# Pairs of token tiles on one Trainium2 core: first-layer sums formed by TensorE in PSUM instead of by VectorE

## The chip, the cores and the metric

One core of one Trainium2 chip (trn2). The metric is the device time of one launch in microseconds (us). The kernel before takes 569.94 us (median of three runs, 569.79 to 570.28).

## The reference

The program is one retention block (linear attention with decay) whose output, 1536 tokens by 512 values, goes through two MLPs of the same size. The change is in the MLPs alone. Cut to what matters:

```python
def _moe_ref(x, w_in, w_out):              # x 1536x512, w_in 512x2048, w_out 2048x512
    h = np.maximum(x @ w_in, 0.0)
    return (h * h @ w_out).astype(np.float32)

def _moe2_ref(x, w_in, w_out):
    h = x @ w_in
    g = np.maximum(0.01 * h, h)
    return (g @ w_out).astype(np.float32)

def reference(**kwargs):
    ...
    return _moe2_ref(x=_moe_ref(x=x, **moe_kwargs), **moe2_kwargs)
```

The weights arrive as 64-bit floats, and the kernel turns them into 32-bit ones itself.

## The kernel before

**Stages.** After the retention block (up to about 62 us of the span) the two MLPs run one after the other, `l` = 0 (squared Relu) and `l` = 1 (leaky Relu). Each is cut into four slices `s` of 512 hidden values, and a stage (l,s) takes all 1536 tokens through its slice: the first layer (`first`, `first_pair`), the activation, and the second layer (`second`, `second_last`), whose results of the slices are added up in DRAM (`keep`, the tiles `spill`). Tokens stand in three tiles of 512 columns. Every fp32 operand is split into a high and a low part of TensorE's type float32r (`split`, L69 copy on ScalarE, L70 remainder on VectorE), and a product of two operands is three matmuls: high by high, high by low, low by high. All matmuls of the MLPs are issued at one line, L531, in `three`; each streams 512 columns.

**Pairs.** In seven of the eight stages the first layer of token tiles 0 and 1 is done by `first_pair` as a 2x2 block product with seven products instead of eight (Winograd's form of Strassen's scheme). The 256 hidden values of each half `h` are the blocks A11 to A22 of the weights (128 rows of the result each), the two tiles' halves are the blocks B11 to B22; S1 to S4 are sums of weight blocks (`weight_sums`, L426 to L431, tiles `sw`), T1 to T4 sums of token blocks (`token_sums`, tiles t2, t3, t4, T1 in place of a block of tile 1). One product is six matmuls into one PSUM bank. A stage has 14 products (seven for each of two halves), always both halves of a product one behind the other. I number the pair stages 1 to 7: (0,1), (0,2), (0,3), (1,0), (1,1), (1,2), (1,3).

**What follows a product.** Before, ScalarE copies A11·B11 out of its bank (L607) into a scratch tile `s1`, and five adds on VectorE for each half (`plus`, L601) form the sums in scratch tiles from the other banks; TensorE itself adds two products into one bank three times (S3·T3 on S2·T2, A12·B21 on A11·B11, S4·B22 on S1·T1). `put` then activates each of the four result blocks (i,t) of a half. For l = 0 a block in scratch gets max(x,0)·x on VectorE (L464), the high part by a copy on ScalarE (L465); a block read from its bank gets Relu, square, square on ScalarE (L467 to L469). For l = 1 both parts come from leaky Relus on ScalarE (L471, L472). The low part is always a subtraction on VectorE (L473), into g0l or g1l, which the second layer reads as weights of tokens 0 or 1.

**Order.** TensorE's order is written out by hand: it is that of the program. SP's (the DMA queue of loads) is by hand in the retention block alone. VectorE, ScalarE and GpSimd get their order from a scheduler that goes by priority, mostly the place in the program; `tc.high_priority(offset=400)` around the adds and around `put` for tile 0 lets them go ahead of work up to that far earlier. An engine takes its instructions strictly in that order, so a waiting instruction holds what is queued behind it.

**Weight conversion.** Between the products the program converts the next weights. A generator `converting` does one piece of 128x1024: ScalarE takes the absolute value (L111) of the raw 64-bit words once their load has landed, VectorE works on it in four steps (L112, L113, L115, L118), of which L118 is the last to read the raw buffer; `fetch` then loads the next piece into it (two raw buffers, 1 MB for a load, issued on SP at L66). For first-layer weights the sums L426 to L429 follow. Once the place in the program allows it (`opened`), ScalarE copies the high part (L135) and VectorE forms the low one (L137). `convert` takes one step of this at every `yield True` of the MLP code; at `yield False` none. So the `yield` values in `first_pair` set where in the program the conversion steps stand:

```python
        for room in part:
            if room is not False:
                convert()
```

Of scratch tiles (`plain`, tag f) there are nine, of the tiles hb that a piece is converted in two, and all eight PSUM banks rotate through `bank()`.

## Time and profile before

| | |
|---|---|
| median of three runs (lowest, highest) | 569.94 us (569.79, 570.28) |
| the profiled execution's own time | 569.29 us |
| its span in the trace | 567.3 us |
| TensorE busy, matmuls | 558.4 us, 98% of the span |
| VectorE busy | 415.6 us, 73% |
| ScalarE busy | 290.6 us, 51% |
| GpSimd busy | 89.8 us, 16% |
| share of TensorE in the chain that ended last | 95%, L531 alone 88% |
| granted clock of TensorE in the profile's slices | nine tenths or more of full speed in all 40 |
| read from and written to HBM | 49.81 and 22.03 MB |

The span is the stretch from the first to the last instruction in the trace; the execution's own time is 1.99 us longer. The stages begin, in us from the start of the span, at 128.02, 190.58, 253.14, 315.83, 378.39, 440.95 and 503.51 for the seven pairs.

### The profile page before, as it was taken

How to read it: one execution, taken by the hardware profiler on the slowest of the kernel's cores; microseconds unless marked ns; L12 is line 12 of the kernel's file. 1: busy time of each engine (PE TensorE's matmuls, PEld its weight loads, DVE VectorE, ACT ScalarE, POOL GpSimd, SP SyncE). 2: the span in 40 equal slices, each digit the busy share in tenths (PEclk: the TensorE clock that was granted, in tenths of full speed). 3: DMA queues.
4: the chain of work that ended last, by engine and by line, in shares of the span. 5: the costliest groups of instructions: out<-in, count | busy, mean ns of one | idle time of the engine just before them, and what ended most of it. 6: DMA issues, size and time to landing. Idle time of an engine off the chain costs nothing.

```text
span 567.3 us, 8188 instructions
## 1 busy us (share of the span) xinstructions
PE 558.4 (98%) x3159; PEld 470.7 (83%) x3159; DVE 415.6 (73%) x613; ACT 290.6 (51%) x450; POOL 89.8 (16%) x101
## 2 busy tenths in 40 slices
PE   7999999999999999999999999999999999999997
PEld 6889888888888888888888888888888888888897
DVE  3678899999955596819999996729563673629877
ACT  2344689553673445733557565454562374436510
POOL 3759100000113102120000000000203011220132
PEclk9999999999999999999999999999999999999999
DMA  8998544536337627394514224442729514460434
GB/s 177 243 211 189 188 148 150 186 149 189 98 47 193 104 76 148 85 194 112 185 29 139 75 91 132 121 175 77 133 61 210 115 20 55 66 83 1 166 133 149
DMA packets 68472, 72.37 MB, mean 128 GB/s; under 512 B 39753, under 2 KB 43857, under 8 KB 68433
## 3 DMA queue, kind: packets, MB, share of 16 engines
q1 hardware_dynamic: 60848, 58.87, 34.7%
q0 software_dynamic: 6912, 12.59, 15.3%
q8 instruction: 25, 0.41, 0.3%
q10 hardware_dynamic: 672, 0.39, 0.2%
q14 instruction: 15, 0.11, 0.1%
HBM read 49.81 MB, written 22.03 MB: 127 GB/s over the span
## 4 chain that ended last, share of the span: by engine, by line
PE 95%; DMA 2%; POOL 1%; SPq 1%; ACT 1%; issue 0%; DVE 0%; ACTq 0%; POOLq 0%
PE ps L531 88%; PE ps L299 2%; PE ps L350 1%; PE ps L282 1%; DMA raw<-in_moe_w_in 1%; PE ps L348 1%; PE ps L323 1%; DMA q<-in_q 1%; SPq L66 1%; POOL kd L317 0%; POOL qS L292 0%; ACT kT L286 0%; ACT qT L286 0%; PE ps L273 0%; ACT xhi L69 0%
## 5 line engine op out<-in xcount | busy, mean ns | idle before, releaser
L650 POOL DMA_DIRECT2D spill<-f x48 | 42.5, 886 | 404.6 <-ACT f L646 258.9
L531 PE MATMUL ps<-xhi,w1h 128*128 128x512 f32 x216 | 84.1, 390 | 0.0
L531 PE MATMUL ps<-xhi,w1l 128*128 128x512 f32 x216 | 84.0, 389 | 0.0
L531 PE MATMUL ps<-xlo,w1h 128*128 128x512 f32 x216 | 84.0, 389 | 0.0
L646 ACT COPY f<-ps 128x512 f32<-128x512 f32 x72 | 42.0, 584 | 74.4 <-PE ps L531 74.0
L137 DVE TENSOR_TENSOR w2l<-hb,w2h 128x1024 fp32r<-128x1024 f32 x16 | 19.6, 1227 | 61.4 <-ACT w2h L135 61.0
L601 DVE TENSOR_TENSOR f<-ps,f 128x512 f32<-128x512 f32 x70 | 46.4, 692 | 6.4 <-PE ps L531 6.3
L473 DVE TENSOR_TENSOR g0l<-f,g0h 128x512 fp32r<-128x512 f32 x52 | 35.3, 691 | 21.3 <-ACT f L472 14.6
L531 PEld LDWEIGHTS ps<-xhi,w1h 128*128 128x128 f32 x216 | 40.5, 188 | 8.5 <-issue 0.2
L531 PEld LDWEIGHTS ps<-xhi,w1l 128*128 128x128 f32 x216 | 40.5, 188 | 8.5
L531 PEld LDWEIGHTS ps<-xlo,w1h 128*128 128x128 f32 x216 | 40.5, 188 | 8.3
L111 ACT ACTIVATE hb<-raw 128x1024 f32<-128x1024 f32 x32 | 36.7, 1148 | 15.3 <-DMA raw<-in_moe_w_in 6.5
L118 DVE SCALAR_TENSOR_TENSOR hb<-raw,hb 128x1024 uint16<-128x1024 uint32 x32 | 43.8, 1367 | 0.2
L531 PE MATMUL ps<-g0l,w2h 128*128 128x512 f32 x112 | 43.7, 390 | 0.0
L531 PE MATMUL ps<-g0h,w2h 128*128 128x512 f32 x112 | 43.6, 389 | 0.0
L531 PE MATMUL ps<-g0h,w2l 128*128 128x512 f32 x112 | 43.6, 389 | 0.0
L531 PE MATMUL ps<-t,sw 128*128 128x512 f32 x168 | 40.3, 389 | 0.0
L531 PE MATMUL ps<-w2l,g0h 128*128 128x512 f32 (+1 forms) x104 | 39.6, 381 | 0.0
L531 PE MATMUL ps<-w2h,g0l 128*128 128x512 f32 (+1 forms) x104 | 39.6, 381 | 0.0
L531 PE MATMUL ps<-w2h,g0h 128*128 128x512 f32 (+1 forms) x104 | 39.6, 381 | 0.0
L115 DVE SCALAR_TENSOR_TENSOR hb<-raw,hb 128x1024 uint32<-128x1024 uint32 x32 | 39.2, 1224 | 0.4
L531 PEld LDWEIGHTS ps<-t,sw 128*128 128x128 f32 x168 | 31.5, 188 | 6.5
(188 smaller groups left out, 1227.4 us busy)
## 6 DMA issues: line engine op xcount, KB each, us to landing
raw<-in_moe_w_in SPq DMA_DIRECT2D x16, 1024.0 KB, 5.7
raw<-in_moe_w_out SPq DMA_DIRECT2D x16, 1024.0 KB, 4.8
spill<-f POOLq DMA_DIRECT2D x48, 256.0 KB, 4.1
spill<-f SPq DMA_DIRECT2D x24, 256.0 KB, 3.1
k<-in_k SPq DMA_DIRECT2D x12, 256.0 KB, 4.6
q<-in_q SPq DMA_DIRECT2D x12, 256.0 KB, 5.2
v<-in_v SPq DMA_DIRECT2D x12, 256.0 KB, 5.7
f<-spill SPq DMA_DIRECT2D x12, 256.0 KB, 2.7
```

Of the source, the lines that this page charges most:

```text
L66: return nc.sync.dma_start(dst, src)
L111: nc.scalar.activation(hf, w_hi.bitcast(F32), AF.Abs)
L115: yield ve.scalar_tensor_tensor(out=hb, in0=w_hi, scalar=0xC0000000, in1=hb, op0=ALU.bitwise_and, op1=ALU.bitwise_or)
L118: step = ve.scalar_tensor_tensor(out=half, in0=w_lo, scalar=2.0 ** -29, in1=half, op0=ALU.mult, op1=ALU.add)
L137: yield ve.tensor_tensor(out=lo, in0=hf, in1=hi, op=ALU.subtract)
L282: nc.tensor.transpose(ps[:, p, :], src[:, 2 * p:2 * p + 2, :].rearrange("s h d -> s (h d)"), ident)
L299: nc.tensor.matmul(raw_scores[i][par][:, p, :], kT[i][r, p, :], qT[i][r, p, :], start=True, stop=True)
L473: nc.vector.tensor_tensor(out=glo, in0=r, in1=ghi, op=ALU.subtract)
L531: nc.tensor.matmul(ps, a, b, start=start and n == 0, stop=stop and n == len(ops) - 1, skip_group_check=again)
L601: ve.tensor_tensor(out=out, in0=ps[h, where], in1=other, op=ALU.add)
L646: nc.scalar.copy(f, src)
L650: nc.gpsimd.dma_start(dst, f, accum_op=ALU.add)
```

## The change

In `first_pair` the scratch sum s1 and the five adds go. `seed` copies a finished product from its bank straight into another bank on ScalarE (L606 of the changed kernel): A11·B11 into bank B, and, once S2·T2 has been added on it there, the sum of the two into bank D. TensorE then accumulates in the seeded banks (`start` false): S2·T2 and S3·T3 and later A22·T4 in B, S4·B22 in D. ScalarE copies S1·T1 into a scratch tile p5 (L619), and two adds for each half are left on VectorE (L610): B + p5 into r22 and D + p5 into p5. The order of the products becomes A11·B11, S1·T1, S2·T2, S3·T3, A12·B21, A22·T4, S4·B22, in place of A11·B11, S2·T2, A22·T4, S3·T3, S1·T1, A12·B21, S4·B22. The block (1,0), once made by an add in scratch, is now read from bank B; for l = 0 that goes by a Relu and a square on ScalarE (L464, L465) and a product r·r on VectorE (L466). A few tiles change their names (`home`, the tag in `weight_sums`), and in the last stage "sums" is opened two products later. In the changed file the old lines L464 to L473 of `activate` stand at L468 to L477, L531 at L535, L646 at L650.

```diff
--- before.py
+++ after.py
@@ -141,7 +141,7 @@
             rb = cv.tile([P, 4 * CW], U32, tag="rb", name="rb")
             w = hf.rearrange("p (k i m f) -> p k i m f", k=2, i=2, m=2)
             blocks = {(i, j): w[:, j, i] for i in range(2) for j in range(2)}
-            yield from weight_sums(key, f"t{h + 2}", blocks, rb.bitcast(F32))
+            yield from weight_sums(key, f"t{2 * h + 2}", blocks, rb.bitcast(F32))
 
     def convert(pin=False):
         for piece in list(at_work):
@@ -448,7 +448,7 @@
                 split(xhi[1][:, j], xlo[1][:, j], a)
                 continue
             if j == 0:
-                tag = {2: "t2", 4: "t3", 3: "t4"}[n]
+                tag = f"t{n}"
                 tt[n] = late.tile([P, 2, 2, TT], F32R, tag=tag, name=tag)
             split(tt[n][:, 0, j], tt[n][:, 1, j], src)
 
@@ -459,8 +459,12 @@
                 nc.vector.tensor_tensor(out=of[k], in0=xhi[t][:, k], in1=xlo[t][:, k], op=ALU.add)
         token_sums(j)
 
-    def activate(l, src, r, ghi, glo):
-        if l == 0 and src is r:
+    def activate(l, src, r, ghi, glo, product=False):
+        if l == 0 and product:
+            nc.scalar.activation(r, src, AF.Relu)
+            nc.scalar.square(ghi, r)
+            nc.vector.tensor_tensor(out=r, in0=r, in1=r, op=ALU.mult)
+        elif l == 0 and src is r:
             nc.vector.scalar_tensor_tensor(out=r, in0=src, scalar=0.0, in1=src, op0=ALU.max, op1=ALU.mult)
             nc.scalar.copy(ghi, r)
         elif l == 0:
@@ -475,7 +479,7 @@
 
 
     whole, tsum = {}, {}
-    home = ("t4", "sw0", "sw1")
+    home = ("t3", "sw0", "sw1")
 
     def by_blocks(x):
         return x.rearrange("q (h j) (p t c) -> q j t h p c", j=2, p=2, t=2)
@@ -576,7 +580,7 @@
         }
         for n in (2, 3, 4):
             x[f"T{n}"] = (tt[n][:, 0], tt[n][:, 1])
-        ps, s1, s2, r22 = {}, {}, {}, {}
+        ps, p5, r22 = {}, {}, {}
 
         def product(h, where, a, b, start=True):
             if start:
@@ -594,49 +598,50 @@
                 if last:
                     activate_last(t, m, src)
                 else:
-                    activate(l, src, r, g[t][0][:, m], g[t][1][:, m])
-
-        def plus(h, out, where, other):
+                    activate(l, src, r, g[t][0][:, m], g[t][1][:, m], (i, t) == (1, 0))
+
+        def seed(h, where, other):
+            ps[h, where] = bank()
             with tc.high_priority(offset=400):
-                ve.tensor_tensor(out=out, in0=ps[h, where], in1=other, op=ALU.add)
+                nc.scalar.copy(ps[h, where], ps[h, other])
+
+        def plus(h, out, where):
+            with tc.high_priority(offset=400):
+                ve.tensor_tensor(out=out, in0=ps[h, where], in1=p5[h], op=ALU.add)
 
         both = range(2)
         for h in both:
-            b = product(h, "A", "A11", "B11")
-            s1[h] = plain()
-            nc.scalar.copy(s1[h], b)
+            product(h, "A", "A11", "B11")
+            seed(h, "B", "A")
             yield True
         for h in both:
-            product(h, "B", "S2", "T2")
-            s2[h] = plain()
-            plus(h, s2[h], "B", s1[h])
+            p5[h] = plain()
+            nc.scalar.copy(p5[h], product(h, "C", "S1", "T1"))
             yield True
         for h in both:
-            product(h, "D", "A22", "T4")
+            product(h, "B", "S2", "T2", False)
+            seed(h, "D", "B")
             yield True
-        if last:
-            opened.add(("sums", l, s))
         for h in both:
             product(h, "B", "S3", "T3", False)
             r22[h] = plain()
-            plus(h, r22[h], "B", s1[h])
-            plus(h, s1[h], "D", r22[h])
-            put(h, s1[h], s1[h], 1, 0)
-            yield last
-        for h in both:
-            product(h, "C", "S1", "T1")
-            plus(h, r22[h], "C", r22[h])
+            plus(h, r22[h], "B")
             yield True
         for h in both:
             put(h, product(h, "A", "A12", "B21", False), plain(), 0, 0)
             yield last
         for h in both:
-            product(h, "C", "S4", "B22", False)
-            plus(h, s2[h], "C", s2[h])
+            put(h, product(h, "B", "A22", "T4", False), plain(), 1, 0)
+            yield last
+        if last:
+            opened.add(("sums", l, s))
+        for h in both:
+            product(h, "D", "S4", "B22", False)
+            plus(h, p5[h], "D")
             yield last
         for h in both:
             put(h, r22[h], r22[h], 1, 1)
-            put(h, s2[h], s2[h], 0, 1)
+            put(h, p5[h], p5[h], 0, 1)
         if last:
             sums_last(0)
             sums_last(1)
```

The number of matmuls, of loads and of stores is the same in both. The next listings show how the order of instructions moves, before and then changed, with the tile numbers of the two programs (they differ between them) and the engines each instruction waits for.

ScalarE in the fourth pair stage (1,0), first before, then changed, then the matmuls of TensorE in the changed kernel that wait there. ps_3062 is bank A of half 0, ps_3069 bank B; ps_3075 and ps_3082 are those of half 1; ps_3113 and ps_3124 are bank D, ps_3088 and ps_3098 bank C of the two halves; raw_2949 and raw_3016 are the two raw buffers.

```order
L607 COPY f_3069<-ps_3062 128x512 [waits PE_49,Activation_49]
L135 CAST w2h_3071<-hb_2983 128x1024 [waits DVE_49]
L607 COPY f_3082<-ps_3075 128x512 [waits PE_49]
L69 CAST xhi2_2972<-f_3036 128x512 [waits DVE_49]
L111 ACTIVATE hb_3084<-raw_2949 128x1024 [waits DMAHW4_49,DVE_49,Activation_49]
L111 ACTIVATE hb_3124<-raw_3016 128x1024 [waits DMAHW6_49,DVE_49,Activation_49]
L471 ACTIVATE g0h_3058<-f_3069 128x512 [waits DVE_49]
```

```order
L606 COPY ps_3069<-ps_3062 128x512 [waits PE_49]
L135 CAST w2h_3071<-hb_2983 128x1024 [waits DVE_49]
L606 COPY ps_3082<-ps_3075 128x512 [waits PE_49]
L69 CAST xhi2_2972<-f_3036 128x512 [waits DVE_49]
L111 ACTIVATE hb_3084<-raw_2949 128x1024 [waits DMAHW4_49,DVE_49,Activation_49]
L619 COPY f_3087<-ps_3088 128x512 [waits PE_49]
L619 COPY f_3097<-ps_3098 128x512 [waits DMASW1_49,PE_49]
L111 ACTIVATE hb_3126<-raw_3016 128x1024 [waits DMAHW6_49,DVE_49,Activation_49]
L606 COPY ps_3113<-ps_3069 128x512 [waits PE_49]
L606 COPY ps_3124<-ps_3082 128x512 [waits PE_49]
L475 ACTIVATE g1h_3060<-f_3135 128x512 [waits DVE_49]
```

```order
L535 MATMUL ps_3069<-t2_2825,sw_2734 128x512 [waits Activation_49]
...
L535 MATMUL ps_3082<-t2_2825,sw_2769 128x512 [waits Activation_49]
...
L535 MATMUL ps_3069<-t3_2833,sw_2734 128x512 [waits Activation_49]
...
L535 MATMUL ps_3082<-t3_2833,sw_2769 128x512 [waits Activation_49]
```

Behind the second L111 stood an L471; now the two copies into bank D stand there, and the first matmuls of S2·T2 (rows on t2) and S3·T3 (rows on t3) wait for ScalarE.

VectorE in the second pair stage (0,2), first before, then changed. hb_2087 and hb_2127 (hb_2129 in the changed kernel) are the two pieces in conversion, rb their weight sums, ps_2090, ps_2100 and ps_2072 banks B.

```order
L112 TENSOR_SCALAR hb_2087<-hb_2087 128x1024 [waits Activation_49]
L113 TENSOR_SCALAR hb_2087<-hb_2087 128x1024 [waits DVE_49]
L115 SCALAR_TENSOR_TENSOR hb_2087<-raw_1926,hb_2087 128x1024 [waits DMAHW1_49,DVE_49]
L601 TENSOR_TENSOR f_2097<-ps_2090,f_2072 128x512 [waits DMASW5_49,DMASW0_49,DMAHW6_49,PE_49,Activation_49]
L601 TENSOR_TENSOR f_2107<-ps_2100,f_2085 128x512 [waits DMASW1_49,DMASW6_49,PE_49,Activation_49]
L118 SCALAR_TENSOR_TENSOR hb_2087<-raw_1926,hb_2087 128x1024 [waits DVE_49]
L112 TENSOR_SCALAR hb_2127<-hb_2127 128x1024
L426 TENSOR_TENSOR rb_2255<-hb_2087 128x256 [waits DVE_49]
L113 TENSOR_SCALAR hb_2127<-hb_2127 128x1024 [waits DVE_49]
L427 TENSOR_TENSOR rb_2255<-hb_2087 128x256
L115 SCALAR_TENSOR_TENSOR hb_2127<-raw_1966,hb_2127 128x1024 [waits DMAHW2_49,DVE_49]
L601 TENSOR_TENSOR f_2136<-ps_2090,f_2072 128x512 [waits DMASW7_49,DMAHW3_49,DMASW2_49,PE_49]
```

```order
L115 SCALAR_TENSOR_TENSOR hb_2087<-raw_1926,hb_2087 128x1024 [waits DMAHW1_49,DVE_49]
L112 TENSOR_SCALAR hb_2129<-hb_2129 128x1024 [waits Activation_49]
L118 SCALAR_TENSOR_TENSOR hb_2087<-raw_1926,hb_2087 128x1024 [waits DVE_49]
L113 TENSOR_SCALAR hb_2129<-hb_2129 128x1024 [waits DVE_49]
L426 TENSOR_TENSOR rb_2255<-hb_2087 128x256 [waits DVE_49]
L115 SCALAR_TENSOR_TENSOR hb_2129<-raw_1966,hb_2129 128x1024 [waits DMAHW2_49,DVE_49]
L427 TENSOR_TENSOR rb_2255<-hb_2087 128x256
L118 SCALAR_TENSOR_TENSOR hb_2129<-raw_1966,hb_2129 128x1024 [waits DVE_49]
L428 TENSOR_TENSOR rb_2255<-rb_2255,hb_2087 128x256
L429 TENSOR_TENSOR rb_2255<-hb_2087,rb_2255 128x256 [waits DVE_49]
L610 TENSOR_TENSOR f_2138<-ps_2072,f_2090 128x512 [waits DMASW5_49,DMASW0_49,DMAHW6_49,PE_49,Activation_49]
L468 SCALAR_TENSOR_TENSOR f_2138<-f_2138 128x512 [waits DVE_49]
```

The adds that stood between the steps are gone; the first add left, L610, stands behind the whole second piece and the sums L428 and L429 of the first.

ScalarE in the same stage, the outputs, first before, then changed. ps_2065 and ps_2078 are bank A of the two halves, ps_2072 and ps_2085 bank B in the changed kernel; g0h is the high part of tile 0, g1h that of tile 1.

```order
L111 ACTIVATE hb_2127<-raw_1966 128x1024 [waits DMAHW2_49,DVE_49]
L607 COPY f_2085<-ps_2078 128x512 [waits DMASW4_49,PE_49]
L465 CAST g0h_2061<-f_2072 128x512 [waits DVE_49]
L465 CAST g0h_2061<-f_2085 128x512 [waits DVE_49]
L467 ACTIVATE f_2178<-ps_2065 128x512 [waits DMASW1_49,PE_49]
L468 ACTIVATE g0h_2061<-f_2178 128x512 [waits Activation_49]
L469 ACTIVATE f_2178<-f_2178 128x512 [waits Activation_49]
L467 ACTIVATE f_2189<-ps_2078 128x512 [waits DMASW2_49,PE_49]
L468 ACTIVATE g0h_2061<-f_2189 128x512 [waits Activation_49]
L465 CAST g1h_2063<-f_2136 128x512 [waits DVE_49]
```

```order
L606 COPY ps_2116<-ps_2072 128x512 [waits PE_49]
L606 COPY ps_2127<-ps_2085 128x512 [waits PE_49,Activation_49]
L469 CAST g1h_2063<-f_2138 128x512 [waits DVE_49]
L471 ACTIVATE f_2156<-ps_2065 128x512 [waits DMASW7_49,PE_49]
L472 ACTIVATE g0h_2061<-f_2156 128x512 [waits Activation_49]
L469 CAST g1h_2063<-f_2147 128x512 [waits DVE_49]
L473 ACTIVATE f_2156<-f_2156 128x512 [waits Activation_49]
L471 ACTIVATE f_2167<-ps_2078 128x512 [waits DMASW0_49,PE_49]
L464 ACTIVATE f_2178<-ps_2072 128x512 [waits DMASW1_49,PE_49]
L472 ACTIVATE g0h_2061<-f_2167 128x512 [waits Activation_49]
L465 ACTIVATE g0h_2061<-f_2178 128x512 [waits Activation_49]
L473 ACTIVATE f_2167<-f_2167 128x512 [waits Activation_49]
```

Tile 1's casts (g1h) and the reads of bank B by L464 now stand between the outputs of tile 0, and the copies into bank D ahead of them.

## Rows read from the trace of the kernel before

**Rows 1.** Profile page, part 1 and part 5 (busy us, mean ns; idle before).

```profile
PE 558.4 (98%) x3159; PEld 470.7 (83%) x3159; DVE 415.6 (73%) x613; ACT 290.6 (51%) x450; POOL 89.8 (16%) x101
...
L601 DVE TENSOR_TENSOR f<-ps,f 128x512 f32<-128x512 f32 x70 | 46.4, 692 | 6.4 <-PE ps L531 6.3
```

**Rows 2.** Waits of the weight loads (us in total, times, longest us).

```profile
PEld ps L531 <- DVE g0l L473: 0.2, 1, 0.2
```

**Rows 3.** Timeline, TensorE, fourth pair stage (start us, us, instruction).

```profile
318.55 2.88 PE L531 MATMUL ps<-t,sw 128*128 128x512 f32 x12
...
323.99 1.30 PE L531 MATMUL ps<-t,sw 128*128 128x512 f32 x5
```

**Rows 4.** Timeline, all engines, around TensorE's one wait in the MLPs.

```profile
306.31 0.71 DVE L473 TENSOR_TENSOR g0l<-f,g0h 128x512 fp32r<-128x512 f32 x1
306.86 0.39 PE L531 MATMUL ps<-g0h,w2h 128*128 128x512 f32 x1
307.07 0.19 PEld L531 LDWEIGHTS ps<-g0l,w2h 128*128 128x128 f32 x1 [0.25 <-DVE g0l L473]
307.41 0.40 PE L531 MATMUL ps<-g0h,w2l 128*128 128x512 f32 x1
```

**Rows 5.** Timeline, first copy of the seventh pair stage.

```profile
504.65 0.39 PE L531 MATMUL ps<-xhi,w1l 128*128 128x512 f32 x1
...
505.13 0.59 ACT L607 COPY f<-ps 128x512 f32<-128x512 f32 x1 [0.83 <-PE ps L531]
```

**Rows 6.** Timeline, ScalarE, fourth pair stage.

```profile
324.40 1.15 ACT L111 ACTIVATE hb<-raw 128x1024 f32<-128x1024 f32 x1 [2.32 <-DVE hb L112]
```

**Rows 7.** Timeline, VectorE and SP's queue, fourth pair stage.

```profile
316.58 0.69 DVE L70 TENSOR_TENSOR xlo<-f,xhi 128x512 fp32r<-128x512 f32 x1
317.18 1.37 DVE L118 SCALAR_TENSOR_TENSOR hb<-raw,hb 128x1024 uint16<-128x1024 uint32 x1
318.62 0.38 SPq L66 DMA_DIRECT2D raw<-in_moe_w_in  x1
```

**Rows 8.** Profile page, part 6 (issues, KB each, us to landing).

```profile
raw<-in_moe_w_in SPq DMA_DIRECT2D x16, 1024.0 KB, 5.7
```

**Rows 9.** Timeline, VectorE, second pair stage.

```profile
194.63 1.23 DVE L115 SCALAR_TENSOR_TENSOR hb<-raw,hb 128x1024 uint32<-128x1024 uint32 x1
195.77 1.28 DVE L601 TENSOR_TENSOR f<-ps,f 128x512 f32<-128x512 f32 x2
196.97 1.34 DVE L118 SCALAR_TENSOR_TENSOR hb<-raw,hb 128x1024 uint16<-128x1024 uint32 x1
198.19 0.69 DVE L112 TENSOR_SCALAR hb<-hb 128x1024 f32<-128x1024 f32 x1
198.79 0.42 DVE L426 TENSOR_TENSOR rb<-hb 128x256 f32<-128x256 f32 x1
199.12 0.69 DVE L113 TENSOR_SCALAR hb<-hb 128x1024 uint32<-128x1024 uint32 x1
```

**Rows 10.** Timeline, ScalarE, second pair stage's outputs.

```profile
208.18 0.64 ACT L468 ACTIVATE g0h<-f 128x512 fp32r<-128x512 f32 x1
208.72 0.61 ACT L465 CAST g1h<-f 128x512 fp32r<-128x512 f32 x1
209.23 0.62 ACT L469 ACTIVATE f<-f 128x512 f32<-128x512 f32 x1
```

**Rows 11.** Timeline, TensorE, second layer after the second pair stage.

```profile
210.53 0.39 PE L531 MATMUL ps<-g0l,w2h 128*128 128x512 f32 x1
...
211.89 0.39 PE L531 MATMUL ps<-g0l,w2h 128*128 128x512 f32 x1
```

**Rows 12.** Timeline, ScalarE, first pair stage.

```profile
128.98 1.15 ACT L111 ACTIVATE hb<-raw 128x1024 f32<-128x1024 f32 x1
130.04 0.57 ACT L646 COPY f<-ps 128x512 f32<-128x512 f32 x1
...
132.80 1.16 ACT L111 ACTIVATE hb<-raw 128x1024 f32<-128x1024 f32 x1 [1.71 <-DMA raw<-in_moe_w_in]
```

## The prediction

> **What bounds the kernel now.** I read the page's busy shares first: TensorE's matmuls fill 98% of the span, VectorE is at 73% and ScalarE at 51% [rows 1]. The chain that ended last is TensorE's for 95%. The next view is the list of what weight loads wait for. In the whole of the MLPs it has one entry with a real wait, 0.2 us once, for VectorE's low part g0l [rows 2]. In TensorE's timeline twelve matmuls take from 318.55 to 321.27, so one starts every 0.2267 us, and a product of six takes 1.36 us [rows 3]. This goes on from 62.6 to 563.5 us.
>
> What a reader is to see is that nothing can be won here. The change leaves the number of matmuls as it is, so the busy time that VectorE loses (42 of its 70 adds at 0.692 us, 29 us [rows 1]) and the time that ScalarE gains (28 more copies at about 0.59, 16.5 us, and six activations) both lie beside a full TensorE. At most the 0.1 us of the one wait could come back. What is left to ask is where TensorE now waits for an engine that it did not wait for before.
>
> **What a late operand costs.** The one wait gives the price. VectorE's g0l ends at 307.02. The weight load that reads it was due when the matmul ahead of it started, at 306.86, and started at 307.07: 0.05 after its operand, 0.21 late. The matmuls at 306.86 and 307.41 stand 0.55 apart for two steps of 0.227, so 0.10 was lost [rows 4]. A load that is late by d thus costs d − 0.115. From the start of a bank's last matmul to ScalarE's copy out of it pass 0.48 us, and the copy takes 0.59 [rows 5].
>
> The Trainium skill ("TensorE: Matmul & The Clock Gate", part 2, "Step-by-step: what each phase is for") says that TensorE pulls weight loads ahead of matmuls in flight, which alone stay in order. The rows have a load held by the wait, not just the matmul behind it. If the load went ahead and only the matmul were held, each of the seven waits below would cost some 0.11 us less, an estimate of 4.0 us in place of the sum of 4.8; I go by the row.
>
> **Part 1, the copy into bank D in the fourth pair stage.** In every pair S2·T2 for half 0 is the fifth product and S3·T3 for half 0 the seventh. Between them lies one product, 1.36 us, in which ScalarE must copy bank B to bank D, since S3·T3 then goes on in B. The copy starts 0.48 after S2·T2's last matmul and takes 0.59; with the 0.05 it leaves 0.24 us before S3·T3's first load is due, 0.36 with what a load tolerates. That is enough only if ScalarE is free.
>
> In the fourth pair it is not. In the changed order the second L111, on raw_3016, stands ahead of both copies into bank D. Before, that L111 started at 324.40 and had idled 2.32 us [rows 6]; nothing urgent was behind it. The row names L112 as its releaser, but what came last is the load: VectorE's L118 frees the raw buffer when it ends at 318.55, SP issues the next load at 318.62 [rows 7], and it takes 5.7 us [rows 8], to 324.3. None of this is moved by the change. So the copy starts one L111 step later, 1.06 us (from 128.98 to 130.04 [rows 12]), at 325.46, ends at 326.05, and S3·T3's load can start at 326.10. It is due one matmul ahead of S3·T3's first, which stood at the seventh product's place, 323.99 [rows 3]: at 323.76. That is 2.34 late, **2.2 us** of stall. The second half's copy ends 0.6 later and its matmuls come 1.36 later, so it adds nothing. In the other six pairs no L111 that waits for a load stands right ahead of the copies into D; I take 0 there, with the 0.36 of slack as cover.
>
> **Part 2, outputs of pairs 2 and 3 (l = 0).** Before, the adds stood between the conversion steps. Now the first add, L610, stands behind the whole second piece. From the end of L115 at 195.77 [rows 9] VectorE runs two L112 and L113 steps of 0.60, one L115 of 1.14 (194.63 to 195.77), two L118 of 1.22, and four of the small sums at 0.33 to 0.42 (L426 0.33, L428 and L429 depend on one another): 1.20 + 1.14 + 2.44 + 1.45 = 6.2 us, to 202.0 [rows 9]. S3·T3 has been readable since 200.3, so the add is 1.7 late. Five VectorE steps of 0.60 to 0.70 follow (add, max·x, add, a low part that waits for ScalarE, max·x), to 205.4.
>
> Only then can ScalarE cast tile 1's second part, and behind that cast stand eight more instructions ahead of the last square on bank B. ScalarE's steps are 0.51 to 0.54 us [rows 10]: from 205.45 to 209.7, and the square ends at 210.3. VectorE's r·r and low part for half 0 stand in the middle of this and end at 210.54; those for half 1 need the square, then 0.6 for r·r, 0.6 for an add and 0.69 for the low part, to 212.34.
>
> The second layer's matmuls on those low parts stood at 210.53 and 211.89 [rows 11], their loads due one step of 0.227 before, at 210.30 and 211.66. The first can start at 210.59, 0.29 late, stall 0.18. The second is due at 211.84 by then and can start at 212.39, 0.55 late, stall 0.43. **0.6 us** for a pair, and pair 3 has the same order: **1.2**. Bounds: none if the chain ends 0.5 sooner, 1.4 if it is as late as pair 1's.
>
> **Part 3, outputs of pair 1.** The same chain, but here the second L111 waits for its load until 132.80 [rows 12], and ends at 133.95: VectorE's clump starts 5.97 us into the stage instead of 5.19 in pair 2. All of it is 0.78 later: **1.4 us**.
>
> **Costed at nothing.** Copies into bank B: between A11·B11 and S2·T2 of the same half lie three products, 4.1 us, against 0.48 + 0.59. The p5 copies stand behind them. For l = 1 (pairs 5 to 7, and the outputs of 4) a block costs two leaky Relus and one subtraction, so two squares and two r·r of the chain in part 2 fall away, 1.2 us of VectorE and 1.1 of ScalarE, against 0.6 of stall: 0.5 us of cover and more. The transfers, SP and GpSimd are the same in number; the two raw loads of w_out that now stand closer on SP's queue were never waited for. Renamed tiles cost nothing.
>
> **The sum.** 2.2 + 1.2 + 1.4 = 4.8 us. The profiled execution took 569.29 us for a span of 567.3; it would be 574.1. The median of the runs is 569.94, 0.65 above it, so the forecast is **574.7 us**; its own range is 573.2 to 576.5 (parts 2 and 3 between half and twice 0.6 a pair).
>
> **The rivals.**
> - Only part 1 (0.17). VectorE has fewer adds in front, and 0.6 us is a tenth of a chain of twenty instructions whose steps I took from another order. If each step were 0.05 shorter, parts 2 and 3 would vanish for pairs 2 and 3, and nearly so for pair 1: 569.9 + 2.2 = 572.1.
> - Only parts 2 and 3 (0.08). The load in the fourth pair lands 2.2 us sooner, by 322.1. For this L118 must end at 316.35 instead of 318.55; its neighbours ahead are subtractions of the tokens [rows 7], none of the adds that go. 569.9 + 2.6 = 572.5.
> - The copies cost more than the row (0.11). No row shows ScalarE writing a bank. As a bound I take the longest ScalarE row of the conversion, 1.15 us [rows 12], for 0.59. Then each copy into D is 0.56 later: pair 4 costs 0.56 more, and each of the other six 0.56 − 0.36 = 0.2, together 1.8: 576.5. From below, the 0.48 and 0.59 of rows 5 could shrink by little and would win nothing. The Trainium skill ("ScalarE: Activation LUTs", "Step-by-step: what each stage is for") says that ScalarE's writes to PSUM are faster than to SBUF; no row here shows it, and by it this rival would fall.
> - No change (0.06), the other side: VectorE, relieved of 29 us [rows 1], runs ahead of its old times by more than the 2.2 us at L118 in pair 4 and the 0.6 to 1.4 at the first L610. The point from which it decides is 316.35 for that L118. Against it, VectorE's steps there follow TensorE's results and ScalarE's L111, not its own backlog. 569.9. Nothing makes it faster than that by a measurable amount.
>
> **How the numbers follow.** Forecast 0.58, rivals 0.17, 0.08, 0.11 and 0.06. A difference of 0.2%, 1.14 us, is about what a measurement of this kernel can tell from none. All cases but the last are slower than that: slower 0.93, within it 0.06, faster 0.01. The range takes in the rivals at 572.1 and 576.5 with their bounds: 571.7 to 577.1.
>
> **What would show it.** The list of waits of the weight loads gets one long entry for ScalarE's copy L606, about 2.3 us, at 323.8 plus what came before, with an L111 that ended just ahead of the copy. It gets five or six entries for g0l at the starts of the second layers after pairs 1 to 3, up to 0.9 us in pair 1. VectorE's share falls to about 68%, ScalarE's rises to 54 or 55%. First to last matmul of the MLPs gets longer by 4.8 us of 500.9. It would be wrong if the copies into D are late in all seven pairs, if the list has no entry for L606, or if the second L111 of pair 4 starts before 322.

## The result, and the profile after

The changed kernel takes 574.69 us (median of four runs, 574.22 to 575.25) against 570.11 us for the kernel before, run beside it: a ratio of 1.0080 with a 95% interval of 1.0063 to 1.0098. The forecast was 574.7. The profiled execution took 574.97 us for a span of 573.0.

The engines' busy time in the profile after, which answers to [rows 1]:

```profile
PE 562.0 (98%) x3159; PEld 471.8 (82%) x3159; DVE 391.8 (68%) x571; ACT 307.5 (54%) x484; POOL 89.5 (16%) x101
```

VectorE is relieved by 23.8 us (415.6 to 391.8, 68% of the span); the 29 reckoned took each add at the length of its row, and rows of 0.7 us stand 0.60 apart where VectorE has no gap. ScalarE does more (54%), and TensorE still fills 98% of a span that is 5.7 us longer. The same count of matmuls, 2328 of the MLPs, now takes 506.12 us from the first to the last start instead of 500.94. In the list of what weight loads waited for [rows 2], these two stand in place of the one:

```profile
PEld ps L535 <- DVE g0l L477: 3.5, 6, 1.2
PEld ps L535 <- ACT ps L606: 2.9, 3, 2.1
```

Nine waits instead of one. The timeline of the weight loads says where each is (start of the load, its duration or that of the run of loads it begins, and in brackets the idle time before and what ended it):

```profile
135.65 1.23 PEld L535 LDWEIGHTS ps<-t,sw 128*128 128x128 f32 x6 [0.54 <-ACT ps L606]
137.14 1.00 PEld L535 LDWEIGHTS ps<-t,sw 128*128 128x128 f32 x5 [0.26 <-ACT ps L606]
150.02 0.19 PEld L535 LDWEIGHTS ps<-g0l,w2h 128*128 128x128 f32 x1 [1.21 <-DVE g0l L477]
151.82 0.19 PEld L535 LDWEIGHTS ps<-g0l,w2h 128*128 128x128 f32 x1 [0.56 <-DVE g0l L477]
213.20 0.19 PEld L535 LDWEIGHTS ps<-g0l,w2h 128*128 128x128 f32 x1 [0.31 <-DVE g0l L477]
215.00 0.19 PEld L535 LDWEIGHTS ps<-g0l,w2h 128*128 128x128 f32 x1 [0.56 <-DVE g0l L477]
276.41 0.19 PEld L535 LDWEIGHTS ps<-g0l,w2h 128*128 128x128 f32 x1 [0.29 <-DVE g0l L477]
278.21 0.19 PEld L535 LDWEIGHTS ps<-g0l,w2h 128*128 128x128 f32 x1 [0.58 <-DVE g0l L477]
329.57 1.45 PEld L535 LDWEIGHTS ps<-t,sw 128*128 128x128 f32 x7 [2.06 <-ACT ps L606]
```

The first two lie in pair 1, the next six at the starts of the second layers after pairs 1, 2 and 3, the last in pair 4. What each stage lost is seen in its length, from the first matmul of a pair stage to that of the next. Before, a pair stage took 62.56 us, the third 62.69 (it held the one wait of [rows 4]). I list how much longer than that each was, here and in all the runs that follow (pair 7 is as long as before in all but the run with the copy made twice):

| kernel | pair 1 | pair 2 | pair 3 | pair 4 | pairs 5, 6 | MLPs, first to last matmul |
|---|---|---|---|---|---|---|
| before | 0 | 0 | 0 | 0 | 0, 0 | 500.94 |
| changed | 2.08 | 0.66 | 0.49 | 1.94 | 0, 0 | 506.12 |
| L111 behind copies, pair 4 | 2.06 | 0.60 | 0.58 | 0.00 | 0, 0 | 504.20 |
| casts behind tile 0 | 0.43 | 0.00 | -0.11 | 1.83 | 0, 0 | 503.10 |
| no copy into D | 2.28 | 0.66 | 0.53 | 0.00 | 0, 0 | 504.42 |
| copy into D twice | 1.40 | 0.63 | 0.56 | 4.16 | 0.24, 0.23 | 509.25 |
| all three held | 0.00 | 0.00 | -0.13 | 0.00 | 0, 0 | 500.85 |
| adds first, pair 1 | 0.35 | 0.53 | 0.41 | 1.88 | 0, 0 | 504.10 |
| adds first, pairs 1 to 3 | 0.25 | 0.00 | -0.11 | 1.83 | 0, 0 | 502.93 |
| L111 behind copies, pair 1 | 0.95 | 0.62 | 0.54 | 1.76 | 0, 0 | 504.82 |

In the changed kernel the four stages make 5.17 us (of pair 1's 2.08, 0.55 fall in the pair's own products and 1.52 in the second layers behind it), all of the 5.18 by which the MLPs are longer. The rest of the span's 5.7 us lies ahead of them: the MLPs' first matmul came at 63.14 us instead of 62.60. In the ten profiles of this study this start lies anywhere from 62.50 to 63.44, whatever the kernel, so I count it for nothing. In part it goes with the clock granted in the retention block: where that was 1.00 on the mean from 10 to 62 us (three profiles) the start is 62.50 to 62.67, and where it was lowest (0.93, two profiles) 63.39 and 63.44. Differences of the medians agree with the table to some 0.6 us only, in the run with two copies to 0.9.

**Pair 4.** ScalarE's timeline, which answers to [rows 6], and then VectorE and SP's queue, which answer to [rows 7]:

```profile
325.65 1.08 ACT L619 COPY f<-ps 128x512 f32<-128x512 f32 x2
327.89 1.15 ACT L111 ACTIVATE hb<-raw 128x1024 f32<-128x1024 f32 x1 [1.17 <-DMA raw<-in_moe_w_in]
328.93 1.06 ACT L606 COPY ps<-ps 128x512 f32<-128x512 f32 x2
```

```profile
320.82 1.39 DVE L118 SCALAR_TENSOR_TENSOR hb<-raw,hb 128x1024 uint16<-128x1024 uint32 x1
322.28 0.38 SPq L66 DMA_DIRECT2D raw<-in_moe_w_in  x1
```

This is what the forecast said: L118 frees the raw buffer (320.82 + 1.39), SP issues the load at 322.28, L111 waits for it (1.17 us idle) until 327.89, and only behind it, at 328.93, come the two copies into bank D. Their wait for TensorE is long over. The load of S3·T3 starts at 329.57, after 2.06 us of waiting.

**Pairs 1 to 3.** VectorE in pair 2 (compare [rows 9]), then ScalarE (compare [rows 10]):

```profile
204.29 0.42 DVE L429 TENSOR_TENSOR rb<-hb,rb 128x256 f32<-128x256 f32 x1
204.63 0.68 DVE L610 TENSOR_TENSOR f<-ps,f 128x512 f32<-128x512 f32 x1
...
207.34 0.69 DVE L468 SCALAR_TENSOR_TENSOR f<-f 128x512 f32<-128x512 f32 x1
...
214.27 0.68 DVE L477 TENSOR_TENSOR g0l<-f,g0h 128x512 fp32r<-128x512 f32 x1
```

```profile
208.06 0.62 ACT L469 CAST g1h<-f 128x512 fp32r<-128x512 f32 x1 [0.20 <-DVE f L468]
...
212.26 0.63 ACT L465 ACTIVATE g0h<-f 128x512 fp32r<-128x512 f32 x1
```

The first add, L610, starts at 204.63, directly behind the last steps of the conversion and of the weight sums. The second max·x (L468) runs from 207.34. ScalarE's second cast (208.06) waits for it, with tile 0's L473 and all the squares but one behind it; the last square starts at 212.26, and the last low part of the half at 214.27. The load that reads it comes at 215.00.

### The profile page after: what moved, and what is told of

It reads as the page before. It is cut to its first block, busy times and chain, and to the rows that moved or that the text cites. A ratio compares the mean times of both kernels' runs of the same rounds, so it can differ in the third digit from the quotient of the medians.

```text
span 573.0 us, 8172 instructions
## 1 busy us (share of the span) xinstructions
PE 562.0 (98%) x3159; PEld 471.8 (82%) x3159; DVE 391.8 (68%) x571; ACT 307.5 (54%) x484; POOL 89.5 (16%) x101
## 4 chain that ended last, share of the span: by engine, by line
PE 62%; DVE 19%; DMA 7%; ACT 7%; issue 4%; SPq 0%; POOL 0%; ACTq 0%; DVEq 0%; POOLq 0%
PE ps L535 56%; DMA raw<-in_moe_w_in 5%; DVE hb L118 3%; DVE hb L115 2%; ACT hb L111 2%; DMA raw<-in_moe_w_out 2%; PE ps L282 1%; PE ps L299 1%; DVE t L70 1%; DVE hb L112 1%; DVE g0l L477 1%; PE ps L350 1%; DVE f L777 1%; DVE hb L113 1%; DVE f L459 1%
## 5 line engine op out<-in xcount | busy, mean ns | idle before, releaser
L535 PE MATMUL ps<-xhi,w1h 128*128 128x512 f32 x216 | 84.2, 390 | 0.0
L535 PE MATMUL ps<-xhi,w1l 128*128 128x512 f32 x216 | 84.0, 389 | 0.0
L535 PE MATMUL ps<-xlo,w1h 128*128 128x512 f32 x216 | 84.0, 389 | 0.0
L651 ACT COPY f<-ps 128x512 f32<-128x512 f32 x72 | 41.9, 584 | 77.6 <-PE ps L535 77.3
L477 DVE TENSOR_TENSOR g0l<-f,g0h 128x512 fp32r<-128x512 f32 x52 | 35.5, 690 | 39.6 <-ACT f L476 26.2
L535 PEld LDWEIGHTS ps<-xhi,w1h 128*128 128x128 f32 x216 | 40.5, 188 | 8.6 <-issue 0.2
L535 PEld LDWEIGHTS ps<-xhi,w1l 128*128 128x128 f32 x216 | 40.5, 188 | 8.4
L535 PEld LDWEIGHTS ps<-xlo,w1h 128*128 128x128 f32 x216 | 40.5, 188 | 8.4
L535 PE MATMUL ps<-g0l,w2h 128*128 128x512 f32 x112 | 44.3, 396 | 1.2 <-DVE g0l L477 0.8
L111 ACT ACTIVATE hb<-raw 128x1024 f32<-128x1024 f32 x32 | 36.5, 1143 | 14.7 <-DMA raw<-in_moe_w_in 8.9
L118 DVE SCALAR_TENSOR_TENSOR hb<-raw,hb 128x1024 uint16<-128x1024 uint32 x32 | 43.6, 1362 | 0.3
L535 PE MATMUL ps<-g0h,w2l 128*128 128x512 f32 x112 | 43.7, 390 | 0.0
L535 PE MATMUL ps<-g0h,w2h 128*128 128x512 f32 x112 | 43.6, 389 | 0.0
L535 PE MATMUL ps<-t,sw 128*128 128x512 f32 x168 | 40.0, 391 | 1.8 <-ACT ps L606 1.6
L535 PE MATMUL ps<-w2l,g0h 128*128 128x512 f32 (+1 forms) x104 | 39.6, 381 | 0.0
L535 PE MATMUL ps<-w2h,g0l 128*128 128x512 f32 (+1 forms) x104 | 39.6, 381 | 0.0
L535 PE MATMUL ps<-w2h,g0h 128*128 128x512 f32 (+1 forms) x104 | 39.6, 381 | 0.0
L115 DVE SCALAR_TENSOR_TENSOR hb<-raw,hb 128x1024 uint32<-128x1024 uint32 x32 | 39.2, 1226 | 0.4
L535 PEld LDWEIGHTS ps<-t,sw 128*128 128x128 f32 x168 | 31.3, 188 | 9.3 <-ACT ps L606 2.9
L535 PE MATMUL ps<-xhi,sw 128*128 128x512 f32 x112 | 36.7, 389 | 0.0
```

Source lines behind the costliest of these rows:

```text
L111: nc.scalar.activation(hf, w_hi.bitcast(F32), AF.Abs)
L115: yield ve.scalar_tensor_tensor(out=hb, in0=w_hi, scalar=0xC0000000, in1=hb, op0=ALU.bitwise_and, op1=ALU.bitwise_or)
L118: step = ve.scalar_tensor_tensor(out=half, in0=w_lo, scalar=2.0 ** -29, in1=half, op0=ALU.mult, op1=ALU.add)
L477: nc.vector.tensor_tensor(out=glo, in0=r, in1=ghi, op=ALU.subtract)
L535: nc.tensor.matmul(ps, a, b, start=start and n == 0, stop=stop and n == len(ops) - 1, skip_group_check=again)
L651: nc.scalar.copy(f, src)
```

## The experiments

Each is the changed kernel with one edit. They tell apart the waits by their causes: which instruction stands in front of a copy, which one makes the low parts late, and whether the waits found are the whole loss.

### The second L111 of pair 4 behind the copies

```diff
-        nc.scalar.activation(hf, w_hi.bitcast(F32), AF.Abs)
+        step = nc.scalar.activation(hf, w_hi.bitcast(F32), AF.Abs)
+        if key == (1, 1, 0, 1):
+            tc.keep_in_program_order(step)
```

`keep_in_program_order` holds an instruction behind what its engine was given before it; in the program this L111 already stands behind the copies, and only the scheduler had moved it ahead.

> Only the second L111 of the fourth pair stage is held behind the two copies into bank D in ScalarE's order; the same values are computed. Theory (the copy stands behind a conversion step that waits for its load): the 2.0 us wait for L606 in the fourth pair goes and nothing takes its place there, 574.7 - 1.9 = 572.8 us; the eight other waits of the changed kernel stay as they are. Rival (the copies into D are slow or late by themselves, or the conversion held back makes weights late): a wait stays in the fourth pair or comes up in its second layers, 574.2 or more.

Measured: 573.19 us (571.92 to 573.8), ratio to before 1.0055 (1.0038 to 1.0072). Pair 4 is as long as before to 0.01 us, the MLPs are 1.92 us shorter than the changed kernel's. ScalarE in pair 4 and what weight loads waited for:

```profile
326.06 0.57 ACT L608 COPY ps<-ps 128x512 f32<-128x512 f32 x1
327.42 0.57 ACT L608 COPY ps<-ps 128x512 f32<-128x512 f32 x1 [0.79 <-PE ps L537]
327.90 1.16 ACT L111 ACTIVATE hb<-raw 128x1024 f32<-128x1024 f32 x1
```

```profile
PEld ps L537 <- DVE g0l L479: 3.6, 6, 1.2
PEld ps L537 <- ACT ps L608: 0.8, 2, 0.5
```

The copies into D now start when TensorE has delivered (326.06 and 327.42), L111 after them at 327.90. That is 8.84 us into the stage, some 0.6 us later than its load, which landed 8.10 us into the stage, would have let it start; the delay costs TensorE nothing. The wait of 2.1 us is gone from the list, and the other eight stay.

### Tile 1's casts behind tile 0's outputs

```diff
-            nc.scalar.copy(ghi, r)
+            tc.keep_in_program_order(nc.scalar.copy(ghi, r))
```

> In stages with squared Relu, ScalarE's casts of tile 1's parts (L469) are held behind all of tile 0's outputs; the same values are computed. Theory (tile 0's low parts are late because ScalarE waits at a cast for VectorE's late add, and tile 0's outputs are queued behind it): all six waits for g0l after pairs 1 to 3 go, 1.5 + 0.6 + 0.6 = 2.6 us, so 572.1 us; the waits for L606 in pairs 1 and 4 stay. Rival (VectorE's conversion clump alone makes the low parts late, or ScalarE has too much to do): waits for g0l of over 0.3 us stay, 573.5 or more.

Measured: 571.53 us (eight runs, 571.29 to 572.51), ratio 1.0033 (1.0023 to 1.0043). ScalarE in pair 2, and the list of waits, which has no entry for g0l any more:

```profile
208.49 0.63 ACT L465 ACTIVATE g0h<-f 128x512 fp32r<-128x512 f32 x1
209.02 0.60 ACT L469 CAST g1h<-f 128x512 fp32r<-128x512 f32 x1
```

```profile
PEld ps L535 <- ACT ps L606: 2.7, 3, 1.9
```

VectorE's adds are as late as in the changed kernel, but the squares no longer stand behind a cast that waits for them. Pair 2 began at 190.92 here and at 193.21 in the changed kernel; the last square starts 17.57 us into the stage (208.49) instead of 19.05 (212.26). All six waits for g0l are gone, after pair 1 as well. So the late add alone delays only tile 1, which is not needed yet; it costs TensorE something through the cast that ScalarE puts in front of tile 0.

### No copy into bank D

```diff
-            seed(h, "D", "B")
...
-            product(h, "D", "S4", "B22", False)
+            product(h, "D", "S4", "B22")
```

> The copies into bank D are left out and S4 B22 starts its bank afresh, so block (0,1) of every pair lacks the products that the copy carried. Theory: the three waits for L606 go (1.9 us in pair 4, 0.5 in pair 1), nothing else moves: 574.7 - 2.4 = 572.3 us. Rival (writes of ScalarE into PSUM slow TensorE or ScalarE in general): all pairs get shorter, 571.5 or less.

Measured: 573.19 us (572.56 to 573.58), ratio 1.0054 (1.0037 to 1.0071). Half a miss. Pair 4's wait goes, and pairs 5 and 6 are not shorter, so the copies themselves cost nothing where they are in time. But pair 1 does not get better, and one wait for L606 is left there:

```profile
136.09 1.92 PEld L535 LDWEIGHTS ps<-t,sw 128*128 128x128 f32 x9 [0.73 <-ACT ps L606]
```

L606 is now only the copy into bank B. I had taken both waits in pair 1 for late copies into D. The load at 135.65 in the changed kernel's list is that of S2·T2, half 1, the sixth product. It started 7.08 us into the stage; the product's place was 5 x 1.36 = 6.80, so its load was due one step earlier, at 6.57. It waits for the copy into bank B. ScalarE in pair 1 of the changed kernel shows why (compare [rows 12]):

```profile
133.99 1.12 ACT L111 ACTIVATE hb<-raw 128x1024 f32<-128x1024 f32 x1 [2.31 <-DMA raw<-in_moe_w_in]
135.01 0.59 ACT L606 COPY ps<-ps 128x512 f32<-128x512 f32 x1
...
136.47 0.61 ACT L606 COPY ps<-ps 128x512 f32<-128x512 f32 x1
```

L111 waits for its load until 133.99 and holds the copy into half 1's bank B (135.01), the p5 copies and the copy into D (136.47) back one after the other.

### The same L111 in pair 1

```diff
+        if key == (0, 2, 0, 1):
+            tc.keep_in_program_order(step)
```

> Only the second L111 of the first pair is held behind both copies into bank B; the same values are computed. Theory (the two waits for L606 in pair 1 are both due to this L111, which waits for its load ahead of the copy into half 1's bank B): both go, 0.5 us less in the trace; the waits for g0l after pair 1 stay at 1.2 and 0.6 us, since VectorE's steps still start from this L111. Rival (the copies into D are late in pair 1 for want of time by themselves): one wait of 0.2 to 0.3 us for L606 stays.

Measured: 573.2 us in one execution. Both waits for L606 in pair 1 are gone. ScalarE in pair 1:

```profile
131.10 0.60 ACT L608 COPY ps<-ps 128x512 f32<-128x512 f32 x1
...
132.99 1.16 ACT L111 ACTIVATE hb<-raw 128x1024 f32<-128x1024 f32 x1
```

The copy into half 1's bank B now runs at 131.10 and L111 stands behind the first p5 copy, at 132.99. The waits for g0l did not stay as I had expected: the first one after pair 1 was 0.63 us instead of 1.21. Here the load that L111 waits for landed sooner: L111 started 4.89 us into the stage, in the changed kernel's profile 5.42, and VectorE's steps follow from there. That time differs from profile to profile (4.78 before, 5.23 and 5.11 in the two runs with the adds first, 5.40 in the first experiment, 5.61 without the copies into D). The L118 that frees the buffer stands at the end of a stretch of 32 us or more in which VectorE has no gap of over 0.05 us, so it comes when VectorE's own backlog is done, not at a fixed point of TensorE's stage. In the eight profiles that have a short last gap there, SP issues the load 32.15 to 32.23 us after the gap's end, so what varies is when the backlog starts. This is read from the traces; no run tried it.

### Each copy into D twice

```diff
             seed(h, "D", "B")
+            with tc.high_priority(offset=400):
+                nc.scalar.copy(ps[h, "D"], ps[h, "B"])
```

> Each copy into bank D is made twice, so that it ends 0.53 us later; the same values are computed. Theory (a copy into D has 0.36 us to spare in pairs 2, 3, 5, 6, 7 and none in 1 and 4): new waits for L606 of some 0.2 us in each of the five, 0.5 more in pair 4 and 0.7 more in pair 1: 574.7 + 2.1 = 576.8 us. Rival (there is more to spare than reckoned, because the copies stand behind work of an idle ScalarE): only pairs 1 and 4 lose, 575.9 or less.

Measured: 578.92 us (578.41 to 579.34), ratio 1.0158 (1.0143 to 1.0173), 2.1 us above what was expected. In the pairs that had room, the expectation holds. In pair 2:

```profile
199.86 0.57 ACT L606 COPY ps<-ps 128x512 f32<-128x512 f32 x1 [0.77 <-PE ps L535]
200.46 0.57 ACT L625 COPY ps<-ps 128x512 f32<-128x512 f32 x1
```

```profile
201.08 2.62 PEld L535 LDWEIGHTS ps<-t,sw 128*128 128x128 f32 x12 [0.32 <-ACT ps L625]
```

The second copy (L625) starts 0.60 after the first and ends at 201.03, and S3·T3's load is 0.32 us idle for it. Pairs 5 and 6 are 0.24 and 0.23 us longer each. A copy that ends 0.60 later costs 0.24, so there was 0.36 to spare, as the forecast had it. In pairs 2 and 3 the stage as a whole is hardly longer than in the changed kernel, because the waits for g0l behind the pair shrank by about as much (in pair 2, 0.23 us more in the pair and 0.27 less behind it). Pair 7 lost more, 1.06 us, because the scheduler put a cast of weight sums between the two copies of half 1.

Pair 1 lost 0.7 us less than in the changed kernel instead of 0.7 more; its L111 came 4.77 us into the stage. With the same order on ScalarE up to there, pair 1 lost 1.40 for an L111 at 4.77, 2.08 for one at 5.42 and 2.28 for one at 5.61 (the run without copies into D): what that stage loses follows its load. Pair 4 is 4.16 us longer, where 1.94 + 0.60 = 2.5 was to be expected. (Of the 2.1 us by which the median is above the expectation, the stages of this profile show 1.0; the rest is the MLPs' late start, at 63.44, and the scatter of the runs around their profiles.) The windows view shows where the rest is (stretch in us, its length, busy time with counts of PE, PEld, DVE, ACT and POOL, then the granted clock, DMA share and GB/s):

```profile
330.00:331.00 1.00, 1.00 (x3) 0.83 (x4) 1.00 (x2) 0.91 (x2) 0.00 (x0) 0.63 0.07 16
331.00:334.00 3.00, 3.00 (x9) 2.31 (x8) 1.70 (x3) 0.66 (x2) 0.00 (x0) 0.55 0.71 206
334.00:337.00 3.00, 3.00 (x15) 2.49 (x14) 2.87 (x4) 1.71 (x4) 0.00 (x0) 1.00 0.36 143
```

After the wait, which ended at 329.90 with a start 2.67 us after the one before, the granted clock is 0.63 and then 0.55 on the mean until 334: most of that time at the lower of TensorE's two levels, 1.2 instead of 2.4 GHz. Seven matmuls stand 0.427 us apart and one 0.40, instead of 0.227, 1.6 us more with the step in which the clock rose again. In the changed kernel the wait in the same place has 2.03 us between starts, and the clock stays at 1.00 behind it:

```profile
330.00:331.00 1.00, 1.00 (x6) 0.82 (x5) 1.00 (x1) 0.00 (x0) 0.00 (x0) 1.00 0.06 16
331.00:334.00 3.00, 3.00 (x14) 2.47 (x14) 2.71 (x5) 1.91 (x4) 0.00 (x0) 1.00 0.60 168
```

### The adds ahead of the conversion

Two runs. In the first the hold took effect in pair 1 only, because the pieces of pairs 2 and 3 are at another step of the program there; the second has it in all three.

```diff
-        yield ve.scalar_tensor_tensor(out=hb, in0=w_hi, scalar=0xC0000000, in1=hb,
-                                      op0=ALU.bitwise_and, op1=ALU.bitwise_or)
+        step = ve.scalar_tensor_tensor(out=hb, in0=w_hi, scalar=0xC0000000, in1=hb,
+                                       op0=ALU.bitwise_and, op1=ALU.bitwise_or)
+        if key in ((0, 2, 0, 1), (0, 3, 0, 1), (1, 0, 0, 1)):
+            tc.keep_in_program_order(step)
+        yield step
...
             nc.scalar.copy(p5[h], product(h, "C", "S1", "T1"))
-            yield True
+            yield (l, s) != (0, 1)
...
             plus(h, r22[h], "B")
-            yield True
+            yield (l, s) != (0, 1) or h == 1
```

(In the first run the two yields are `l == 1` and `l == 1 or h == 1`.)

> In pairs 1 to 3 the last two conversion steps of the second piece (L115, L118) are held behind VectorE's first adds; ScalarE's casts stay in the changed kernel's order; the same values are computed. Theory (the add comes late behind the conversion, and this is what the cast and all behind it wait for): the second max times x ends 1.3 us sooner, so the waits for g0l after pairs 2 and 3 go and at most 0.2 us is left after pair 1: 574.7 - 2.5 = 572.2 us, the waits for L606 in pairs 1 and 4 as they were. Rival (only the place of the casts in ScalarE's order matters): the waits for g0l shrink by less than half, 573.4 or more.

> As the run before it, but the hold now takes effect in all three pairs (before, the two conversion steps stood behind the adds in pair 1 alone, and in pairs 2 and 3 ahead of them as in the changed kernel). ScalarE's order in the outputs is the changed kernel's. Theory: the waits for g0l after pairs 2 and 3 go as the one after pair 1 did; MLPs 2.6 us shorter than the changed kernel's, 572.1 us; the waits for L606 stay. Rival (pair 1's waits went for another reason, its yields): waits of 0.3 and 0.6 us for g0l stay after pairs 2 and 3, 573.2.

Measured: 573.25 us (572.78 to 573.61), ratio 1.0054 (1.0041 to 1.0067), then 572.14 us (571.28 to 572.25), ratio 1.0046 (1.0029 to 1.0062). In the first run the waits for g0l after pair 1 are gone and those after pairs 2 and 3 are as in the changed kernel; in the second all six are gone. The lists of waits, of the first run for g0l and of the second, where L609 is all that is left:

```profile
PEld ps L538 <- DVE g0l L480: 1.6, 4, 0.6
```

```profile
PEld ps L538 <- ACT ps L609: 2.4, 3, 2.0
```

The first run is its own control: the yields are changed in its pairs 2 and 3 too, but the conversion still stands ahead of the adds there, and the waits stay. Its VectorE in pair 2, and then the second run's VectorE in the same pair:

```profile
199.43 1.22 DVE L115 SCALAR_TENSOR_TENSOR hb<-raw,hb 128x1024 uint32<-128x1024 uint32 x1
...
202.78 0.72 DVE L613 TENSOR_TENSOR f<-ps,f 128x512 f32<-128x512 f32 x1
...
205.52 0.69 DVE L471 SCALAR_TENSOR_TENSOR f<-f 128x512 f32<-128x512 f32 x1
```

```profile
200.65 0.69 DVE L613 TENSOR_TENSOR f<-ps,f 128x512 f32<-128x512 f32 x1 [0.56 <-PE ps L538]
...
202.62 1.22 DVE L115 SCALAR_TENSOR_TENSOR hb<-raw,hb 128x1024 uint32<-128x1024 uint32 x1
203.75 0.68 DVE L471 SCALAR_TENSOR_TENSOR f<-f 128x512 f32<-128x512 f32 x1
```

Where the second piece's L115 (199.43), its last step and weight sums stand ahead, the first add (L613 here) comes at 202.78 and the second max·x (L471 here) at 205.52. With L115 behind the adds they come at 200.65, when its product is there, and at 203.75. Pair 2 began at 191.49 and 190.88 in the two, so the second max·x is 1.16 us earlier in the stage (12.87 instead of 14.03), and TensorE's waits go, though ScalarE's order in the outputs is untouched.

So the late add and the cast in front are not rivals but two links of one chain. Either one taken out is enough.

### All three held

The edits of the first, second and fourth experiment together (L111 held for (0,2,0,1) and (1,1,0,1), and the casts).

> Three things together, the same values computed: the second L111 of the fourth pair behind the copies into bank D, the second L111 of the first pair behind both copies into bank B, and tile 1's casts behind tile 0's outputs. Theory (the loss is the sum of these waits and nothing else): no wait of a weight load of over 0.1 us in the pairs or the second layers behind them, first to last matmul of the MLPs as before within 0.2 us (500.9), 569.9 us, no difference to the kernel before. Rival (the 28 copies or the relieved VectorE cost or win something beyond the waits seen so far): off by more than 0.5 us, 570.5 or more, or 569.2 or less.

Measured: 569.85 us (twelve runs, 569.11 to 570.36) against 570.17, ratio 0.9993 (0.9984 to 1.0001). The first to the last matmul of the MLPs is 500.85 us; no weight load of the MLPs waits for ScalarE or VectorE, and what is left for them in the list is the start of the first MLP matmul:

```profile
PEld ps L537 <- issue: 0.2, 1, 0.2
```

Its busy times:

```profile
PE 560.1 (99%) x3159; PEld 473.0 (83%) x3159; DVE 393.0 (69%) x571; ACT 308.0 (54%) x484; POOL 89.3 (16%) x101
```

This kernel has the change's whole work: 22.6 us less of VectorE than before and 17.4 us more of ScalarE. It is neither faster nor slower than the kernel before. The waits were the whole loss, and the relief of VectorE by itself is worth nothing here.

## Why the prediction was right

The time was right, and so was the mechanism of the three parts; of the four terms of the loss one was missing from the sum. Two of the signs were off by it or in size: the list got three entries for L606 and not one, and the longest wait for g0l was 1.21 us, not 0.9.

- *TensorE is full, so nothing can be won.* The kernel with everything held shows it: all of the relief, no gain.
- *Part 1, 2.2 us.* Measured 1.94 in pair 4, at the place and by the instruction named; holding that L111 takes it to 0.00. The load took 5.5 us of the 5.7 reckoned and was waited for until 327.89, 8.28 us into the stage against 8.57 before; the forecast of this part was too large by about these 0.29 us.
- *Part 2, 0.6 us a pair.* Measured 0.66 and 0.49, or 0.62 for the second if the 0.13 is added that the stage before spent on a wait of its own. The chain is that of the forecast link by link: conversion, add, max·x, cast, squares, low part. In pair 2 the first add started 11.42 us into the stage and the last square 19.05; the forecast's times, 202.0 and 209.7 less the 190.58 at which the stage began, are 11.4 and 19.1. (Between that cast and the last square stand seven instructions, not eight; the time for eight steps, 4.2 us, was right.) Taking the add forward or the cast back both end it.
- *Part 3, 1.4 us.* Pair 1 is 2.08 longer, of which 1.52 lie behind the pair, by the starts of the matmuls around the two waits for g0l. That its size hangs on when the L111 in pair 1 starts is borne out by two other runs: with L111 0.53 sooner (held behind the copies) 0.95 was lost behind the pair, with L111 0.65 sooner (each copy twice) 0.91.
- *Costed at nothing: "between A11·B11 and S2·T2 of the same half lie three products, 4.1 us, against 0.48 + 0.59".* This failed in pair 1, where the rest of the 2.08, 0.5 us, lies. The step counted only the copy, not what stands ahead of it on ScalarE, though part 3 rests on the very L111 that does. The copy into D behind it was late too, against the sentence that in the other six pairs no such L111 stands right ahead of them. By the rows of before it would have ended at 132.80 + 1.06 + 0.59 = 134.45, against a load due at 134.59, with 0.1 to spare; in the changed kernel the load was 0.65 us later into the stage, and the spare was gone. In the run with each copy made twice L111 stood in the same place but started at 4.77, and this load did not wait.
- *The price of a late load, d − 0.115.* In the wait at 150.02 the matmul before stands at 148.85, so the load was 1.17 late. By the price that costs 1.06; the starts below give 150.36 − 148.85 = 1.51 for two steps of 0.227, a loss of 1.06:

```profile
148.85 0.39 PE L535 MATMUL ps<-g0h,w2h 128*128 128x512 f32 x1
150.02 0.50 PE L535 MATMUL ps<-g0l,w2h 128*128 128x512 f32 x1 [0.79 <-DVE g0l L477]
150.36 0.40 PE L535 MATMUL ps<-g0h,w2l 128*128 128x512 f32 x1
```

- *The copies are dearer than their row.* They are not: 0.576 us from bank to bank, 0.590 from bank to scratch. This rival falls. The Trainium skill ("ScalarE: Activation LUTs", "Step-by-step: what each stage is for"), by which a write to PSUM is the faster one, agrees in sign, by 0.014 us (0.008 against the 72 copies of L651, at 0.584):

```profile
L606 ACT COPY ps<-ps 128x512 f32<-128x512 f32 x28 | 16.1, 576 | 10.3 <-PE ps L535 10.1
L619 ACT COPY f<-ps 128x512 f32<-128x512 f32 x14 | 8.0, 590 | 4.4 <-PE ps L535 4.4
```

- *The load is held, not just the matmul.* Of the Trainium skill's pull-ahead of weight loads ("TensorE: Matmul & The Clock Gate", "Step-by-step: what each phase is for") the waits here say what [rows 4] did: the load itself carries the wait. If only the matmul were held, the 1.17 us at 150.02 would have cost 1.17 − 0.23 = 0.94, and they cost 1.06. The sum of 4.0 us that the other reading gave is 1.2 below the 5.17 of the stages, but 0.5 of this is the missing term.
- *The rivals without part 1 or with no change* needed L118 of pair 4 to end 2.2 us sooner. It ended 2.60 us into the stage, before 2.71. The reason given, that VectorE's steps there follow TensorE's results and ScalarE's L111 and not its own backlog, does not hold: in both kernels VectorE has no gap of over 0.05 us in the 15 us ahead of the stage and up to that L118. But none of the adds that went stood in this backlog, so it did not move. The rival that parts 2 and 3 vanish fell with their 1.15 and 1.52 us.
- *The inner range.* Halving and doubling parts 2 and 3 gives 573.4 and 577.3, not the 573.2 and 576.5 stated. Nothing hangs on it.

The terms as forecast sum to 4.8, the stages to 5.17 and the medians to 4.58: the missing term and the uncertainty of the medians lie on opposite sides, so the agreement to 0.01 us is luck; the agreement of the three forecast terms, each to 0.3 us, is not.

## What to carry to other kernels

When one engine is full, count a change by the instructions that stand ahead of what that engine will newly wait for, on the engine that delivers it; the busy time saved elsewhere pays nothing. A copy of 0.6 us with 0.36 us to spare is safe until the scheduler puts an instruction in front of it that waits for a transfer, so every such neighbour has to be looked up in the changed order, for each copy separately. Taking work off an engine can make its other work run in a clump: the adds that were removed here had kept the conversion steps apart, and the adds that stayed ended up behind them.

## What the runs showed of the hardware

A wait of TensorE with 2.03 us between matmul starts left the granted clock at 1.00; one with 2.67 us in the same place was followed by some 3 us at the lower level (0.55), with matmuls at 0.427 us, which cost 1.6 us on top of the wait. The drop was seen in this one profile; in the four other runs that kept the wait in pair 4, with 1.84 to 1.96 us between starts, the clock stayed at 1.00 too. Whether a wait of 2.67 us always does this is not shown. In a kernel that lives on a full TensorE a wait that gets 0.6 us longer can so cost 2.2.

Behind a late weight load, the matmul starts with the load (both at 150.02) and the next one 0.34 us later, not 0.23. The first saves 0.227 of the lateness, the second gives 0.11 back: this is what the price of d − 0.115 is made of.
